# Stage B of a Fourier filter on 64x64 array tiles, with its loads and reads rearranged

## The chip, the core and the metric

The kernel runs on one core of a Trainium2 chip. The core has a matrix engine (TensorE, PE in the profile; PEld is its weight load), a vector engine (VectorE, DVE), a scalar engine (ScalarE, ACT), a general engine (GpSimd, POOL) and SyncE (SP), which here only issues transfers. Each engine works through its own list of instructions in order and waits on semaphores. Sixteen DMA engines move data; they take transfers from a queue fed by SyncE (q1 in the profile), one fed by GpSimd (q0), and others. TensorE's products land in PSUM, eight banks of 128 partitions by 512 f32. The metric is the time of one execution in microseconds (us) on the device; lower is better.

## What is computed

```
X = rfft(x, axis=1)                    # x: [8, 3008, 256] f32
y = irfft(X * (filt_r + 1j*filt_i))    # [8, 3008, 256]
t = y.reshape(24064, 256)
out = (relu(t @ w_gate) * (t @ w_val)) @ w_out      # d_ff = 1536
```

Eight batches of 3008 positions with 256 channels go through a global filter in frequency space. The 24064 rows that come out go through a gated feed-forward layer (FFN) of width 1536.

## The kernel before, in words

The Fourier transform of 3008 = 94 x 32 is split in two.

*Stage A* transforms over n1 (94 positions, folded by symmetry) and gives 96 rows (real and imaginary parts of 48 frequencies k1) for each of 32 n2. It writes them to Abuf in DRAM. Batches 0 and 1 do it with full matmuls (`items_a`, psA). Batches 2 to 7 load chunks of x (`load_chunk`, six DMAs for each of four chunks), fold them on GpSimd (`fold_chunk`, six additions or subtractions), and multiply them on sixteen 32x32 tiles of the array (`tiled_a`, psF): tiles of one matmul instruction each, with a `tile_position` that says which rows and columns of the array it uses.

*Stage B* reads Abuf back by frequency (`load_at`, `load_at_tiled`; the tile `at`), transforms over n2, multiplies by the filter and transforms back. One frequency k1 is a 64x64 matrix (32 complex numbers). There are 24 groups g, each with two such matrices on the diagonal of a 128x128 matrix, half of which is zero. `fwd` (in `items_b`) makes psX for two groups with two matmuls; DVE multiplies psX by the real and the imaginary filter (tt and uu); `inv`, two or three calls later, makes psD with four matmuls (I2t with tt, I2u with uu), ACT copies it to dsb, and after six groups SyncE writes dsb to Dbuf in DRAM.

*The last transform* over n1 is joined with the FFN: `load_d` reads Dbuf (dC, four n2 a read, eight reads a batch), and `item_c` makes psY, the FFN's input of 512 rows (a block), copied to yT by ACT and DVE.

*The FFN* takes 47 blocks. Each has 12 steps: `gv` makes psV and psG (two matmuls of 512 columns each); ACT copies psV to vsb, DVE makes prod = relu(psG) x vsb; `o_part` adds a third of an output tile of the block before (four matmuls of 256 columns, psO), copied to osb by ACT in steps 5 and 11 and written out by SyncE.

The order is written out by hand. A table `side` says at which step of the FFN loop which part of the filter of a later batch is put in, after that step's `gv` and `o_part`: `at_step(s, f)`. `end` is the step from which the rest of batch b is counted; it lies five steps before the `item_c` that needs its first rows, and 72 steps before the next batch's. Stage B of a batch starts at `sb0`, 30 steps before `end` (batch 1: step 19), with one `fwd` and one `inv` every second step. The step decides only the place in each engine's list. An instruction runs as soon as its engine has come to it and its waits are met.

PSUM has four tags of two banks: fft, psv, psg and pso. In the FFN loop, psX, psD and psY take turns on the two banks of fft; psV and psG have psv and psg; `tiled_a` takes one bank each of psv and psg and both of fft. SBUF tiles have a number of buffers (`bufs`); a tile waits for the last user of the buffer that it takes over.

Before the loop, stage A of batch 0 and its stage B run alone, then stage A of batch 1 begins inside stage B of batch 0 (`amid`). GpSimd loads the filters and the FFN's weights (`load_vg`, `load_o`). The matrices for stage B are made on the chip: DVE spreads a table into F2 (`place_forward`), TensorE turns F2 into I2t and I2t into I2u (`make_back`).

```
for s, z in ((2, 2), (9, 4), (14, 6)):
    at_step(s, lambda z=z: load_d(0, z, z + 2))
```

This puts the remaining reads of batch 0's Dbuf at steps 2, 9 and 14; batch 1's `load_at` stands at step 5, so behind the first of them in SyncE's list.

Of the kernel before, what the change touches and what calls it, by code (L numbers as in the profile page):

```python
# [41 lines left out]
def _tables():  # L42
# [3 lines left out]
    wa = np.zeros((128, NROW + 2))  # L46
    for a in range(2):
        wa[64 * a:64 * a + 64, NROW + a] = 1.0
# [7 lines left out]
    for hg in range(48):  # L56
        g, a = divmod(hg, 2)
        rows = slice(a * 64, a * 64 + 64)
        f = np.zeros((64, 64))
# [4 lines left out]
        wa[part, 2 * hg] = np.cos(th)  # L64
        if k1 not in (0, 47):
            wa[part, 2 * hg + 1] = -np.sin(th)
            m1[48 * a + g] = 2.0 * np.cos(th) / S
            m1[48 * a + 24 + g] = -2.0 * np.sin(th) / S
# [8 lines left out]
        else:  # L77
            m1[48 * a + g] = np.cos(th) / S
# [15 lines left out]
        f2[lo + 64 * a, g] = f  # L94
# [4 lines left out]
    col = 4 * (8 * (r % 4) + r // 4 % 8) + 2 * (r // 64) + r // 32 % 2  # L99
    perm = np.zeros((128, 128))  # L100
    perm[r, col] = 1.0
# [15 lines left out]
    tab = np.concatenate([f2.reshape(128, -1), perm, swap, own.reshape(128, -1), m1], 1)  # L117
    return wa.astype(np.float32), fold.reshape(128, 128).astype(np.float32), tab.astype(NBF16)
# [3 lines left out]
def kernel(  # L122
# [17 lines left out]
    NZ = 8  # L140
# [4 lines left out]
    wa_h, fold_h, tab_h = _tables()  # L145
# [14 lines left out]
    WA = pro.tile([128, NROW + 2], FP32)  # L160
    WF = consts.tile([128, 4, 32], FP32)
    M1 = consts.tile([NROW, N1], BF16)
    F2 = consts.tile([128, NG, 128], BF16)
    I2t = consts.tile([128, NG, 128], BF16)
    I2u = consts.tile([128, NG, 128], BF16)
# [20 lines left out]
    f2c = tabs[:, 0:NG * 64].rearrange("p (g f) -> p g f", f=64)  # L186
    perm, swap = tabs[:, NG * 64:NG * 64 + 128], tabs[:, NG * 64 + 128:NG * 64 + 256]

    def place_forward():
        for a in range(2):  # L190
            nc.vector.tensor_scalar(F2[:, :, a * 64:a * 64 + 64], f2c,
                                    WA[:, NROW + a:NROW + a + 1], None, op0=ALU.mult)
        nc.vector.tensor_copy(M1, tabs[:NROW, NG * 64 + 512:])

    def make_back(i, q):

        psI = ps.tile([128, 4, 128], FP32, tag=fft_tag(), name="psI")
        gs = slice(4 * q, 4 * q + 4)
        if i == 0:
            for j in range(4):  # L200
                nc.tensor.matmul(psI[:, j], F2[:, 4 * q + j, :], perm, start=True, stop=True)
        else:
            nc.tensor.matmul(psI, swap, I2t[:, gs, :], start=True, stop=True)
        copy = nc.scalar.copy if i == 1 else nc.vector.tensor_copy
        copy((I2t, I2u)[i][:, gs, :], psI)

    def place_own():

        for i, t in enumerate((I2t, I2u)):
            o = NG * 64 + 256 + i * 128  # L210
            nc.vector.tensor_copy(
                t[64:, NG - 2:, :].rearrange("p g (n a c) -> p g n a c", a=2, c=2)[:, :, :, 1, :],
                tabs[64:, o:o + 128].rearrange("p (g n c) -> p g n c", g=2, c=2))
# [54 lines left out]
    def items_a(b):  # L268

        def one(c, j, st):  # L270
            if j == 0:
                st["asb"] = sb.tile([128, NC2 * D], BF16, tag="asb", bufs=4, name="asb")
            psA = ps.tile([128, 512], FP32, tag=fft_tag(), name="psA")
            o = (c * NC2 % NX2) * D + j * 512
            nc.tensor.matmul(psA[0:NROW], WA[:, :NROW], XF[c * NC2 // NX2][:, o:o + 512],  # L275
                             start=True, stop=True)
            dst = st["asb"][:NROW, j * 512:(j + 1) * 512]
            nc.scalar.copy(dst, psA[0:NROW])
            if j == 3:
                nc.sync.dma_start(_ap(Abuf[b], c * NROW * NC2 * D, [[NC2 * D, NROW], [1, NC2 * D]]),  # L280
                                  st["asb"][:NROW])
# [7 lines left out]
    def load_chunk(b, j):  # L289

        xp = XP[(4 * b + j) % 3]
        for q in range(4):
            r, o = 32 * q, 8 * q + 2 * j
            nc.sync.dma_start(xp[r:r + 24, 0:4:2, :],
                              _ap(x, (b * N1 * N2 + o) * D,
                                  [[N2 * D, 24], [47 * N2 * D, 2], [1, 512]]))
        for i in range(2):
            nc.sync.dma_start(xp[:, 2 * i + 1, :],
# [3 lines left out]
    def fold_chunk(b, j):  # L302

        xp = XP[(4 * b + j) % 3]
        t = fs.tile([128, 2, 512], FP32, tag="fold", bufs=2, name="fold")
# [9 lines left out]
    def tiled_a(b, j):  # L315
# [8 lines left out]
        asf = sb.tile([128, NC2 * D], BF16, tag="asb", bufs=4, name="asb")  # L324
# [9 lines left out]
    def load_at_tiled(b):  # L334

        ats[b] = sb.tile([128, NG, D], BF16, tag="at", bufs=1, name="at")
        for rr in range(4):
            for e in range(2):
                nc.sync.dma_start(ats[b][32 * rr:32 * rr + 32, e:NG:2, :],
                                  _ap(Abuf[b], (48 * (rr % 2) + 24 * e + 12 * (rr // 2)) * N2 * D,  # L340
                                      [[D, 32], [N2 * D, 12], [1, D]]))

    GC = 6
    POOL_G = (4, 6, 10, 12, 16, 18)
# [8 lines left out]
    def items_b(b, amid=None):  # L353

        held = []
        st = {}
        lag = 2 if b else 3
        cuts = (0, 6, 12, 18, 24) if b else (0, 6, 12, 18, 22, 24)

        def fwd(g):  # L360
            at = ats[b]
            psX = ps.tile([128, 2, D], FP32, tag=fft_tag(), name="psX")
            for i in range(2):
                nc.tensor.matmul(psX[:, i], F2[:, g + i, :], at[:, g + i, :], start=True, stop=True)  # L364
            tt = sb.tile([128, 2, D], BF16, tag="tt", bufs=4)
            uu = sb.tile([128, 2, D], BF16, tag="uu", bufs=4)
            nc.vector.tensor_tensor(tt, psX, Ftr[:, g:g + 2, :], op=ALU.mult)  # L367
            if b == 0 and g in POOL_G:
                xs = pro.tile([128, 2, D], FP32, tag="xs", bufs=2)
                nc.scalar.copy(xs, psX)  # L370
                nc.gpsimd.tensor_tensor(uu, xs, Fti[:, g:g + 2, :], op=ALU.mult)  # L371
            else:
                nc.vector.tensor_tensor(uu, psX, Fti[:, g:g + 2, :], op=ALU.mult)  # L373
            held.append((g, tt, uu))

        def inv():
            g, tt, uu = held.pop(0)
            if g in cuts:
                st["dsb"] = sb.tile([128, GC, D], BF16, tag="dsb", bufs=4, name="dsb")
                st["g"] = g  # L380
            psD = ps.tile([128, 2, D], FP32, tag=fft_tag(), name="psD")
            for i in range(2):
                nc.tensor.matmul(psD[:, i], I2t[:, g + i, :], tt[:, i], start=True, stop=False)  # L383
                nc.tensor.matmul(psD[:, i], I2u[:, g + i, :], uu[:, i], start=False, stop=True)  # L384
            o = g - st["g"]
            nc.scalar.copy(st["dsb"][:, o:o + 2, :], psD)  # L386
            if g + 2 in cuts:
                nc.sync.dma_start(_ap(Dbuf[b], st["g"] * D, [[NG * D, 128], [1, (o + 2) * D]]),
                                  st["dsb"][:, :o + 2, :])

        for g in range(0, NG, 2):
            def both(g=g):
                fwd(g)
                if amid:
                    amid(g // 2)
                if len(held) > lag:
                    inv()
            yield both
        for _ in range(lag):
            yield inv  # L400
# [3 lines left out]
    def load_d(b, z0=0, z1=NZ):  # L404
        for z in range(z0, z1):
            dC = sb.tile([NROW, 4, D], BF16, tag="dC", bufs=12)
            nc.sync.dma_start(dC, _ap(Dbuf[b], z * 4 * NROW * D,
                                      [[D, NROW], [NROW * D, 4], [1, D]]))
# [14 lines left out]
    def item_c(k, h):  # L423
# [4 lines left out]
        for (o, b, n2, n1, w) in runs(k * W, W):  # L428
            nc.tensor.matmul(psY[:, o:o + w],  # L429
                             dCs[b, n2 // 4][:, n2 % 4, h * 128:(h + 1) * 128], M1[:, n1:n1 + w],  # L430
# [25 lines left out]
    def o_part(blk, s, prods):  # L456
# [9 lines left out]
        if s in (5, 11) or last and s % 3 == 2:  # L466
            t0 = t if last else t - 1
            osb = fs.tile([128, 2, D], FP32, tag="osb", bufs=5)
# [31 lines left out]
    load_x(0, nc.sync, ((0, 0, 2 * q), (0, 2 * q, 4 * q), (1, 0, 2 * q)))  # L500
    nc.sync.dma_start(tabs, nc.inline_tensor(tab_h, name="dft_tab").ap())
# [9 lines left out]
    place_forward()  # L511
    for i, f in enumerate(items_a(0)):
        f()
        if i >= 10:
            make_back(0, i - 10)
        else:
            warm(1, 256)
# [7 lines left out]
    for q in range(6):  # L525
        make_back(1, q)
        warm(3)
# [18 lines left out]
    for f in items_b(0, amid):  # L546
        f()
    load_d(0, 0, 2)
# [12 lines left out]
    def clear_chunks():  # L561
        for i in range(3):
# [9 lines left out]
    for s, z in ((2, 2), (9, 4), (14, 6)):  # L572
        at_step(s, lambda z=z: load_d(0, z, z + 2))
    C_AT = (8, 10)
    at_step(2, clear_chunks)
    for b in range(1, B):
        end = (b * S // W - 1) * NFT + C_AT[0] - 5
        sb0 = 19 if b == 1 else end - 30 | 1
        if b == 1:
            for c in range(4):  # L580
                at_step(5, lambda c=c: load_at(1, c))
        else:
            for j, (l, e) in enumerate(((-66, -41), (-60, -33), (-54, -27), (-40, -17))):
                at_step(sb0 + l, lambda b=b, j=j: load_chunk(b, j))
                at_step(sb0 + l + 1, lambda b=b, j=j: fold_chunk(b, j))
                at_step(sb0 + e, lambda b=b, j=j: tiled_a(b, j))
            at_step(sb0 + e + 4, lambda b=b: load_at_tiled(b))
# [45 lines left out]
```

## Time and profile before

| | us |
|---|---|
| median of 3 runs | 914.34 (913.85 to 916.62) |
| profiled execution | 913.1 |
| its span, first to last instruction | 911.3 |
| TensorE busy | 896.0 |
| VectorE busy | 578.0 |
| ScalarE busy | 500.8 |
| GpSimd busy | 262.4 |
| mean granted TensorE clock | 0.995 of full |

In the page's lists of groups a row gives the line of the kernel, the engine, the operation, what it writes and reads, its shape and how often it ran; then the busy time and the mean of one in ns; then how long the engine stood idle just before, and what ended that. In a timeline a row is start, length, engine, line, operation, tile and count, where equal rows that follow each other are merged. The chain of waits goes back from the last instruction to what released each one; its shares say which engine's work makes up the span. Durations of matmuls overlap, so how far apart they start says more than how long they take.

### The profile page before, as it was taken

Reading aid. Unit: us, or ns where it says so; the run is one execution under the profiler, and the core shown is the slowest. Engines: PE = TensorE matmul, PEld = TensorE weight load, DVE = VectorE, ACT = ScalarE, POOL = GpSimd, SP = SyncE. Lnnn points to the kernel's source line nnn. Section 1 sums busy time; section 2 is a strip of 40 time slices with the busy share of each in tenths; the row PEclk is TensorE's granted clock in tenths of the full one; section 3 lists DMA queues with packets and bytes.
Section 4 is the critical chain, followed back from the end, with each engine's and each line's share of the span. In section 5 each row is a group of like instructions: output and inputs, shape, how many; then the busy total and the mean of one; then the engine's idle time right before and its main releaser. Section 6 shows DMA issues by size and latency. Waiting matters only on the chain.

```text
span 911.3 us, 18044 instructions
## 1 busy us (share of the span) xinstructions
PE 896.0 (98%) x6602; PEld 545.7 (60%) x6602; DVE 578.0 (63%) x875; ACT 500.8 (55%) x893; POOL 262.4 (29%) x181
## 2 busy tenths in 40 slices
PE   8799999999999999999999999999999999999997
PEld 3445665666655666556655566556665566666665
DVE  3737766568655775657755587555865567655553
ACT  4675555555555555555555555555555555555552
POOL 4340174405451074400844017440355300000000
PEclk9899999999999999999999999999999999999999
DMA  9996336444355345452353433525446242231111
GB/s 254 256 252 143 116 122 166 111 90 138 122 153 105 82 150 139 119 117 84 129 168 94 115 111 118 165 76 121 115 134 166 65 106 66 85 78 36 36 31 51
DMA packets 106138, 109.04 MB, mean 120 GB/s; under 512 B 9794, under 2 KB 87362, under 8 KB 105410
## 3 DMA queue, kind: packets, MB, share of 16 engines
q1 hardware_dynamic: 101222, 103.77, 40.7%
q0 software_dynamic: 4512, 3.90, 2.8%
q8 instruction: 52, 0.85, 0.4%
q14 instruction: 36, 0.29, 0.1%
q10 hardware_dynamic: 316, 0.22, 0.1%
HBM read 61.94 MB, written 49.81 MB: 123 GB/s over the span
## 4 chain that ended last, share of the span: by engine, by line
PE 95%; DMA 3%; SPq 0%; ACT 0%; POOL 0%; DVE 0%; issue 0%; ACTq 0%; POOLq 0%
PE psV L445 27%; PE psG L445 27%; PE psO L464 26%; PE psF L321 3%; PE psA L275 3%; PE psY L429 2%; PE psD L383 2%; PE psD L384 2%; PE psX L364 2%; DMA XF<-in_x_dram 1%; DMA Abuf<-asb 1%; DMA at<-Abuf 0%; DMA out_dram<-osb 0%; SPq L178 0%; SPq L478 0%
## 5 line engine op out<-in xcount | busy, mean ns | idle before, releaser
L450 DVE SCALAR_TENSOR_TENSOR prod<-psG,vsb 128x512 bf16<-128x512 f32 x564 | 390.0, 692 | 274.6 <-ACT vsb L448 265.6
L448 ACT CAST vsb<-psV 128x512 bf16<-128x512 f32 x564 | 332.0, 589 | 244.7 <-PE psV L445 206.4
L445 PE MATMUL psV<-yT,WvT 128*128 128x512 bf16 x1128 | 335.9, 379 | 0.9 <-ACT yT L434 0.7
L464 PE MATMUL psO<-WoT,prod 128*128 128x256 bf16 x2256 | 336.4, 273 | 0.0
L445 PE MATMUL psG<-yT,WgT 128*128 128x512 bf16 x1128 | 335.3, 379 | 0.0
L464 PEld LDWEIGHTS <-prod 128*128 128x128 bf16 x2256 | 220.7, 98 | 143.4
L445 PEld LDWEIGHTS <-WgT 128*128 128x128 bf16 x1128 | 110.0, 98 | 133.8 <-issue 0.5
L307 POOL TENSOR_TENSOR fold<-XP 128x1024 f32<-128x1024 f32 x24 | 56.4, 2351 | 404.5 <-DMA out_dram<-osb 170.9
L445 PEld LDWEIGHTS <-WvT 128*128 128x128 bf16 x1128 | 102.3, 98 | 33.1 <-issue 20.9
L386 ACT CAST dsb<-psD 128x512 bf16<-128x512 f32 x96 | 55.9, 588 | 51.7 <-PE psD L384 50.0
L367 DVE TENSOR_TENSOR tt<-psX,Ftr 128x512 bf16<-128x512 f32 x96 | 65.2, 682 | 4.2 <-PE psX L364 4.2
L470 ACT COPY osb<-psO 128x512 f32<-128x512 f32 x92 | 53.9, 586 | 22.7 <-PE psO L464 20.3
L373 DVE TENSOR_TENSOR uu<-psX,Fti 128x512 bf16<-128x512 f32 x90 | 61.3, 681 | 0.0
L308 POOL TENSOR_TENSOR XP<-XP 128x1024 f32<-128x1024 f32 x24 | 56.4, 2349 | 1.9
L384 PE MATMUL psD<-uu,I2u 128*128 128x256 bf16 x192 | 47.6, 276 | 0.6 <-POOL uu L371 0.6
L383 PE MATMUL psD<-tt,I2t 128*128 128x256 bf16 x192 | 47.9, 276 | 0.0
L328 ACT CAST asb<-psF 128x512 bf16<-128x512 f32 x48 | 25.8, 589 | 32.5 <-PE psF L321 32.5
L328 DVE CAST asb<-psF 128x512 bf16<-128x512 f32 x48 | 30.9, 686 | 17.3 <-PE psF L321 14.5
L364 PE MATMUL psX<-at,F 128*128 128x256 bf16 x192 | 37.8, 281 | 3.9 <-DMA at<-Abuf 3.9
L436 DVE CAST yT<-psY 128x512 bf16<-128x512 f32 x47 | 32.0, 681 | 12.9 <-PE psY L429 12.9
L434 ACT CAST yT<-psY 128x512 bf16<-128x512 f32 x47 | 27.5, 586 | 22.7 <-PE psY L429 22.6
L429 PE MATMUL psY<-M,dC 96*128 96x94 bf16 (+18 forms) x604 | 37.5, 198 | 0.0
(64 smaller groups left out, 439.9 us busy)
## 6 DMA issues: line engine op xcount, KB each, us to landing
dC<-Dbuf SPq DMA_DIRECT2D x64, 192.0 KB
XP<-in_x_dram SPq DMA_DIRECT2D x48, 256.0 KB
Dbuf<-dsb SPq DMA_DIRECT2D x31, 384.0 KB
XP<-in_x_dram SPq DMA_DIRECT2D x96, 96.0 KB
Abuf<-asb SPq DMA_DIRECT2D x96, 96.0 KB
at<-Abuf SPq DMA_DIRECT2D x48, 192.0 KB
out_dram<-osb SPq DMA_DIRECT2D x70, 94.0 KB
XF<-in_x_dram SPq DMA_DIRECT2D x12, 256.0 KB
```

The costliest lines, as they stand in the source:

```text
L307: tt(t, xp[:, 0:2], xp[:, 2:4], op=ALU.add)
L308: tt(xp[:, 2:4], xp[:, 0:2], xp[:, 2:4], op=ALU.subtract)
L328: copy(asf[:, :, q, :], banks[q])
L364: nc.tensor.matmul(psX[:, i], F2[:, g + i, :], at[:, g + i, :], start=True, stop=True)
L367: nc.vector.tensor_tensor(tt, psX, Ftr[:, g:g + 2, :], op=ALU.mult)
L373: nc.vector.tensor_tensor(uu, psX, Fti[:, g:g + 2, :], op=ALU.mult)
L383: nc.tensor.matmul(psD[:, i], I2t[:, g + i, :], tt[:, i], start=True, stop=False)
L384: nc.tensor.matmul(psD[:, i], I2u[:, g + i, :], uu[:, i], start=False, stop=True)
L445: nc.tensor.matmul(pt[:, :W], w[:, h, ft * 128:(ft + 1) * 128], yt[:, h, :], start=(h == 0), stop=(h == 1))
L448: nc.scalar.copy(vsb, psV[:, :W])
L450: nc.vector.scalar_tensor_tensor(prod, in0=psG[:, :W], scalar=0.0, in1=vsb, op0=ALU.max, op1=ALU.mult)
L464: nc.tensor.matmul(psO[:, t % 2], prods[ft][:, t * 128:(t + 1) * 128], WoT[:, ft, :], start=(ft == 0), stop=(ft == NFT - 1))
```

## The change

- Stage B works on 64x64 array tiles. F2, I2t and I2u hold 64 columns a group instead of 128 half-empty ones. `fwd(b, i)` does four groups: for each of two halves m, four matmuls on the four quarters of the array, into two banks (psX for e = 0 and e = 1). `inv(b, i)` does four groups with sixteen matmuls into two banks of psv and psg. `product` makes one of the four products of a `fwd`.
- In the FFN loop a batch has seven such places instead of fourteen: for batches 2 to 7 at -40, -35, -28, -23, -16, -11 and -4 from `end`, for batch 1 at -35, -28, -25, -22, -16, -11 and -4. The four products go to that step and the three after it; `inv` of the four groups before stands right behind `fwd`.
- x chunks are loaded from GpSimd's queue, not SyncE's, into four buffers XP instead of three. All four loads and then all four folds stand together at -104 to -100.
- D is read 8 n2 at a time (four dC of two DMAs each, six buffers instead of twelve). dsb holds eight groups, so three writes a batch instead of four. `at` is read with four DMAs instead of eight.
- At the start of the loop, batch 1's `load_at` stands at step 3 and the second read of batch 0's D at step 4.
- F2 is loaded ready made; `make_back_t` and `make_back_u` replace `make_back`, and `place_forward` goes.
- Buffers: asb 4 to 3, dsb 4 to 3, osb 5 to 4, fold 2 to 3, tt and uu 4 to 5.

```diff
-    F2 = consts.tile([128, NG, 128], BF16)
+    F2 = consts.tile([128, NG, 64], BF16)
...
+    def make_back_t(q):
+        psI = [ps.tile([128, 4, 64], FP32, tag=fft_tag(), name="psI") for _ in range(2)]
+        for e in range(2):
+            for a in range(2):
+                for j in range(4):
+                    nc.tensor.matmul(psI[e][64 * a:64 * a + 64, j],
+                                     F2[64 * e:64 * e + 64, 12 * a + 4 * q + j, :],
+                                     perm[64 * e:64 * e + 64], start=True, stop=True,
+                                     tile_position=(64 * e, 64 * a))
...
-        xp = XP[(4 * b + j) % 3]
+        xp = XP[j]
...
-            nc.sync.dma_start(xp[r:r + 24, 0:4:2, :],
+            nc.gpsimd.dma_start(xp[r:r + 24, 0:4:2, :],
...
-            nc.sync.dma_start(xp[:, 2 * i + 1, :],
+            nc.gpsimd.dma_start(xp[:, 2 * i + 1, :],
...
+    def fwd(b, i, es=(0, 1)):
+        for e in es:
+            psXs[b, i, e] = ps.tile([128, 2, D], FP32, tag=fft_tag(), name="psX")
+        for m in range(2):
+            for e in es:
+                for a in range(2):
+                    j = 12 * a + 2 * i + m
+                    nc.tensor.matmul(psXs[b, i, e][64 * a:64 * a + 64, m],
+                                     F2[64 * e:64 * e + 64, j, :],
+                                     ats[b][64 * e:64 * e + 64, j, :], start=True, stop=True,
+                                     tile_position=(64 * e, 64 * a))
+
+    def product(b, i, e, k, pool=False):
+        psX = psXs[b, i, e]
+        p = sb.tile([128, 2, D], BF16, tag=("tt", "uu")[k], bufs=5, name=("tt", "uu")[k])
+        filt = (Ftr, Fti)[k][:, 4 * i + e:4 * i + 4:2, :]
...
+            nc.vector.tensor_tensor(p, psX, filt, op=ALU.mult)
+        tus[b, i, e, k] = p
+
+    def inv(b, i, tags=None, cuts=CUTS):
+        if i in cuts:
+            dsbs[b] = i, sb.tile([128, 2, 4, D], BF16, tag="dsb", bufs=3, name="dsb")
+        i0, dsb = dsbs[b]
+        psD = [ps.tile([128, 2, D], FP32, tag=tags[a] if tags else fft_tag(), name="psD")
+               for a in range(2)]
+        for m in range(2):
+            for k in range(2):
+                for a in range(2):
+                    for e in range(2):
+                        nc.tensor.matmul(psD[a][64 * e:64 * e + 64, m],
+                                         (I2t, I2u)[k][64 * a:64 * a + 64, 4 * i + 2 * m + e, :],
+                                         tus[b, i, e, k][64 * a:64 * a + 64, m],
+                                         start=(k == 0), stop=(k == 1),
+                                         tile_position=(64 * a, 64 * e))
+        o = 2 * (i - i0)
+        for a in range(2):
+            nc.scalar.copy(dsb[:, a, o:o + 2, :], psD[a])
...
-    for s, z in ((2, 2), (9, 4), (14, 6)):
-        at_step(s, lambda z=z: load_d(0, z, z + 2))
+    for s, z in ((4, 1), (9, 2), (14, 3)):
+        at_step(s, lambda z=z: load_d(0, z, z + 1))
...
-                at_step(5, lambda c=c: load_at(1, c))
+                at_step(3, lambda c=c: load_at(1, c))
...
-            for j, (l, e) in enumerate(((-66, -41), (-60, -33), (-54, -27), (-40, -17))):
-                at_step(sb0 + l, lambda b=b, j=j: load_chunk(b, j))
-                at_step(sb0 + l + 1, lambda b=b, j=j: fold_chunk(b, j))
-                at_step(sb0 + e, lambda b=b, j=j: tiled_a(b, j))
+            for j, (l, e) in enumerate(((-104, -74), (-103, -69), (-102, -62), (-101, -57))):
+                at_step(end + l, lambda b=b, j=j: load_chunk(b, j))
+                at_step(end - 100, lambda b=b, j=j: fold_chunk(b, j))
+                at_step(end + e, lambda b=b, j=j: tiled_a(b, j))
...
-        for i, f in enumerate(items_b(b)):
-            at_step(sb0 + 2 * i, f)
-        at_step(sb0 + 27, lambda b=b: load_d(b))
+        for i, l in enumerate((-35, -28, -25, -22, -16, -11, -4) if b == 1 else
+                              (-40, -35, -28, -23, -16, -11, -4)):
+            if i < 6:
+                at_step(end + l, lambda b=b, i=i: fwd(b, i))
+                for h in range(4):
+                    at_step(end + l + h, lambda b=b, i=i, h=h: product(b, i, h // 2, h % 2))
+            if i > 0:
+                at_step(end + l, lambda b=b, i=i: inv(b, i - 1, ("psv", "psg")))
+        at_step(end - 2, lambda b=b: load_d(b))
```

## The prediction

> **What bounds the kernel now.** I read the page's busy shares, then its chain of waits, then windows of the timeline around the places the diff touches.
>
> ```profile
> span 911.3 us, 18044 instructions
> ...
> PE 896.0 (98%) x6602; PEld 545.7 (60%) x6602; DVE 578.0 (63%) x875; ACT 500.8 (55%) x893; POOL 262.4 (29%) x181
> ...
> PE 95%; DMA 3%; SPq 0%; ACT 0%; POOL 0%; DVE 0%; issue 0%; ACTq 0%; POOLq 0%
> ...
> L367 DVE TENSOR_TENSOR tt<-psX,Ftr 128x512 bf16<-128x512 f32 x96 | 65.2, 682 | 4.2 <-PE psX L364 4.2
> ```
>
> TensorE is 95% of the chain, so a matmul fewer is time saved and a new wait of TensorE is time lost. One FFN step with stage B work, from TensorE's timeline:
>
> ```profile
> 202.17 0.38 PE L364 MATMUL psX<-at,F 128*128 128x256 bf16 x2
> 202.39 0.27 PE L383 MATMUL psD<-tt,I2t 128*128 128x256 bf16 x1
> ...
> 202.83 0.59 PE L445 MATMUL psV<-yT,WvT 128*128 128x512 bf16 x2
> ...
> 204.13 0.38 PE L445 MATMUL psV<-yT,WvT 128*128 128x512 bf16 x1
> ```
>
> Six stage B matmuls take 0.66 us (0.109 each); a bare step takes 1.30 (202.83 to 204.13). Stage A already uses array tiles (psF):
>
> ```profile
> 245.19 0.60 PE L464 MATMUL psO<-WoT,prod 128*128 128x256 bf16 x4
> ...
> 245.72 0.61 PE L321 MATMUL psF<-XP,WF 24*32 24x512 f32 x1
> ...
> 246.18 0.59 PE L321 MATMUL psF<-fold,WF 24*32 24x512 f32 x2
> ...
> 246.44 0.59 PE L321 MATMUL psF<-fold,WF 24*32 24x512 f32 x2
> 246.45 0.59 PE L321 MATMUL psF<-XP,WF 24*32 24x512 f32 x1
> 246.97 0.60 PE L445 MATMUL psV<-yT,WvT 128*128 128x512 bf16 x2
> ```
>
> The sixteen tiles do overlap. Getting in costs 0.09 us (four psO at 0.109 end at 245.63, psF starts at 245.72). So does getting out: an untiled f32 pass takes 0.43, so the last psF ends at 246.88 and psV starts at 246.97. A tile's second pass starts 0.45 after its first, 0.026 more than its stream.
>
> The start of the FFN loop: SyncE's queue and TensorE in the timeline,
>
> ```profile
> 61.74 1.14 SPq L407 DMA_DIRECT2D dC<-Dbuf  x2
> 63.04 9.54 SPq L350 DMA_DIRECT2D at<-Abuf  x4
> ```
> ```profile
> 69.67 0.39 PE L429 MATMUL psY<-M,dC 96*128 96x52 bf16 x6
> ```
>
> and packets by queue (q0 GpSimd's, q1 SyncE's) in 66 to 72.5 us, then in 72.5 to 80:
>
> ```profile
> q0 software_dynamic: 1284, 0.64, 71.5%
> q1 hardware_dynamic: 1449, 0.82, 56.3%
> ```
> ```profile
> q1 hardware_dynamic: 4111, 2.04, 116.0%
> ```
>
> The DMA engines are saturated here (their share is 1.11, 1.28 and 1.17 in 60 to 66, to 72.5 and to 80). Block 1's psY at 69.67 reads two dC of 192 KB that stand ahead of batch 1's four at reads; no wait shows.
>
> **Part by part.** The profiled run took 913.1 (span 911.3 and 1.8 around it); the median is 1.2 higher, 914.3. Differences are summed against the profiled run and moved to the median.
>
> *Tiles, batches 1 to 7.* Out go 72 matmuls a batch, 72 x 0.109 = 7.86 us. In come 48 + 96 quarter-array ones in 36 rounds of four, in 7 slots, each with entry and exit of 0.19 and about 0.02 of stagger: 1.44. A round lies between 0.109 (a full-array stream) and 0.218 (two tiles take turns). psF's rows lie far nearer the first, with 0.026 extra at worst; I take 0.120: 36 x 0.120 + 1.44 = 5.76, a gain of 2.10 a batch, **-14.7** over seven. At 0.109 it is -17.5, at 0.135 -10.9, at 0.218 +10.0.
>
> The weight loads have no row: psF's are 32 columns of f32, start 0.007 apart and overlap. The Trainium skill, "TensorEngine Tiling (Array Packing)", Restrictions and Gotchas, says that column tiling switches fast weight load off, and "TensorE: Matmul & The Clock Gate", LDWEIGHTS, gives columns / 1.2 ns. Four loads of 53 ns one after another would make an estimated round of 0.213, and the sum 942 instead of the forecast; no run here shows such a load.
>
> *Batches 2 to 7, the covers.* inv now takes a psv and a psg bank and two dsb copies fall in one step. ACT then owes vsb, at times osb, and two dsb, 4 x 0.59 = 2.36, against a step of 1.30 + 0.93, and catches up in the next step. DVE owes 5 x 0.69 + 4 x 0.68 = 6.2 in the shortest gap of five steps, where TensorE takes 7.4. Banks come free some 0.4 us early: 0. Gone, that cover would cost up to 0.3 a slot.
>
> *Batch 1* has gaps of three steps, twice (-28, -25, -22). There the fourth product stands on DVE in the same step as the next fwd, which needs its bank. From the first slot's step: ACT is in dsb until 3.45, so vsb ends at 4.0; then DVE, a start each 0.60 (as at 33.98, 34.59, 35.19), does prod, product, prod, product, prod, product until 7.75. TensorE is there at 6.3. Wait 1.5, twice: **+3.0** (0 to 4.4).
>
> *Block 1's dC reads move behind the at reads* (at_step 3 before at_step 4; both on SyncE's queue). TensorE comes to psY at step 8, at 69.7 as before, and now needs 3072 packets of at (4 x 384 KB by 512 B) and 768 of dC. By the window rows some 1400 of them have gone at 72.5, and the remaining 2440 at 4111 / 7.5 = 548 per us land at 77.0. That is the low end.
>
> *x loads on GpSimd's queue.* 144 issues leave SyncE (idle or waiting mostly; worth 0) and join GpSimd. Nothing holds them to their steps there: batch 2's 24 stand right behind four memsets (5.29 for three from 60.87, so done at 67.9) and start then, not near 100. They are 1792 packets of 2 KB, at some 0.6 us per issue (GpSimd's DMA rows are 0.50 to 0.75) until 82.3. In 66 to 72.5 the two queues got about equal turns (1284 and 1449 packets); with equal turns at the 314 GB/s of 60 to 66, 2.5 KB a pair and so 122 pairs per us, dC lands near 88. The ends are 77 and 88. The issue pace leaves gaps to q1, so I take 83, midway: TensorE stands still, **+13.3** against 69.7. Behind its waiting psY stand steps 9 to 11 and all of block 1, and ACT and DVE wait for those; batch 1's at, which lands before, is late for nobody.
>
> *Cold clock after that stall.* Before, after 3.93 us idle, TensorE ran at 0.50 from 33.4 to 38.6 us:
>
> ```profile
> 33.40:38.50 5.10, 5.10 (x27) 3.61 (x28) 4.52 (x8) 1.39 (x3) 2.36 (x4) 0.50 0.68 119
> ```
>
> 5.2 us at half is **+2.6**. The Trainium skill, "TensorE: Matmul & The Clock Gate", Part 1, has full rate back after one busy window of about 3.4 us. By that it would be an estimated 1.7 and the sum 0.9 lower.
>
> *asb with three buffers.* Batch 1's last chunk waits for its first chunk's write to land, near 62 (96 packets of 4 KB, begun at 60 behind the dC reads, at the 396 packets of 60 to 66), instead of a copy at 58.2. Four copies and yT later the FFN loop starts near 64.8 instead of 61.9. This +2.9 lies inside the stall above: 0; without the stall it counts.
>
> *Batch 0 and the tables.* F2 comes by DMA instead of two DVE multiplies (618 ns each, off the path). Six groups of four 128-column matmuls (0.22 each) become three tiled groups, 0.19 + 16 x 0.03: +0.4 before the Abuf write. Stage B of batch 0 after the x of batch 1 lands (43.75) loses six inv and two fwd at 0.11 a matmul for tiles: -0.4. Sum 0, within 0.5.
>
> *The rest at 0.* GpSimd's folds: 2 x 2.35 + 4 x 1.27 = 9.8 a chunk, with 3.6 for its loads 53 us a batch, where a batch lasts 110 (first psF 135.9 to 245.7). Loads wait for tiled_a of the batch before, folds stand behind them, and each fold still ends some five steps ahead of its tiled_a. D: last inv at 238.69, psY at 252.18; the write is 512 KB instead of 384 and two reads are needed, about 1 us later, with 2 us to spare and two psF more in between. at in four reads of the same bytes, osb with four buffers (a reuse every 31 us): unseen. If these covers go, TensorE waits at psF or psY once a batch.
>
> Sum: -14.7 + 3.0 + 13.3 + 2.6 = +4.2; 917.3 for the profiled run, **918.5** for the median.
>
> **Rivals.**
> - *The at and dC reads keep their pace beside the x loads* (dC at 77). For it: a DMA of GpSimd's waits for an older one, so few are in flight. Against: equal turns in 66 to 72.5. -14.7 + 3.0 + 7.3 + 2.6 = -1.8: 912.5.
> - *The other side, faster: block 1's reads are there by 72.6,* when TensorE arrives. -14.7 + 3.0 + 2.9 = -8.8: 905.5. It decides at 78.8 us: dC landing before that leaves a gain, after it a loss. Against: 3840 packets must pass first; for: only the queue's order, not the packets, is certain.
> - *Waits per slot in batches 2 to 7* (the fwd, bank or dsb cover gone): 36 slots x 0.3 = +11: 929. Against: 0.4 us in hand.
> - *The tiles take turns* (0.218 a round), the change does not do what it says: +24.7, 943. Against: psF.
>
> **How the numbers follow.** Forecast 0.48 (its own range 912 to 925), first rival 0.22, faster rival 0.13, slot waits 0.12, turns 0.05. From 906 to 929 leaves out about half of the faster rival, the turns and part of the slot waits, together under 0.2. 0.3% is 2.7 us, about what a measurement can tell: the forecast gives 0.01 faster, 0.15 same, 0.32 slower; the first rival 0.09, 0.10, 0.03; the faster one 0.12 and 0.01; the others are slower. Faster 0.22, same 0.26, slower 0.52.
>
> **What would show it.** Right: psY idle some 10 us for DMA dC between 70 and 85 us, GpSimd issuing XP loads from 68, PEclk low just after; two waits of psX for DVE's products in batch 1 of about 1.5; 24 tiles in 0.93 us from psO to psV. Wrong: no idle at psY near 72 (faster rival), rounds of 0.2, or TensorE waiting for banks, psF or psY in each batch.

## The result and the profile after

The changed kernel takes 946.62 us (median of 4 runs, 939.2 to 949.45), the one before 914.1 beside it: 1.0338 times as long, 95% interval 1.0270 to 1.0406. The direction was the forecast one; the forecast was 918.5, and the time lies 17.6 us above its range. The profiled execution took 944.06, its span 942.3 (31.0 more than before). The page's span, busy times and shares of the chain of waits, changed kernel:

```profile
span 942.3 us, 19150 instructions
...
PE 890.0 (94%) x7202; PEld 515.7 (55%) x7202; DVE 567.9 (60%) x873; ACT 497.0 (53%) x890; POOL 352.9 (37%) x326
...
PE 76%; DMA 13%; SPq 2%; DVE 1%; issue 1%; ACT 0%; DVEq 0%
PE psV L461 23%; PE psO L480 22%; PE psG L461 22%; DMA Abuf<-asb 6%; DMA at<-Abuf 4%; PE psF L320 3%; PE psD L390 2%; PE psY L445 2%; DMA dC<-Dbuf 2%; PE psX L361 2%; DMA out_dram<-osb 1%; SPq L422 1%; SPq L337 1%; SPq L329 0%; DVE prod L466 0%
```

TensorE fell from 95% of the chain to 76%, and transfers rose from 3% to 13%: Abuf's writes and the at reads, not dC, have the larger shares. TensorE's waits, changed kernel (total us, times, longest):

```profile
PE psY L445 <- DMA dC<-Dbuf: 22.5, 1, 22.5
PE psX L361 <- DMA at<-Abuf: 11.4, 5, 4.5
PE psX L361 <- DMA out_dram<-osb: 4.9, 3, 3.3
...
PE psX L361 <- DVE uu L376: 2.2, 2, 1.1
```

The first and the last line were forecast. The two in the middle are one thing: the first psX of a batch waits for all of `at`, and the profile names whichever transfer ended last; the 4.5 in the second line is batch 0's own first read, 3.9 in the kernel before. One of a batch's five places that hold 24 tiles, TensorE's timeline:

```profile
220.81 0.60 PE L480 MATMUL psO<-WoT,prod 128*128 128x256 bf16 x4
221.34 0.41 PE L361 MATMUL psX<-at,F 64*64 64x256 bf16 x8
221.59 0.28 PE L390 MATMUL psD<-tt,I2t 64*64 64x256 bf16 x4
221.69 0.28 PE L390 MATMUL psD<-uu,I2u 64*64 64x256 bf16 x4
221.80 0.28 PE L390 MATMUL psD<-tt,I2t 64*64 64x256 bf16 x4
221.91 0.28 PE L390 MATMUL psD<-uu,I2u 64*64 64x256 bf16 x4
222.12 0.60 PE L461 MATMUL psV<-yT,WvT 128*128 128x512 bf16 x2
```

Four quarter tiles start every 0.11 us, the pace of one full matmul before. Places of 24, 16 and 8 tiles without a wait last 0.875, 0.657 and 0.438 in all batches: 0.109 a round and 0.219 for getting in and out. A batch costs 5 x 0.875 + 0.657 + 0.438 = 5.47 instead of 7.86.

The start of the loop, TensorE's and then SyncE's timeline:

```profile
73.36 0.27 PE L445 MATMUL psY<-M,dC 96*128 96x52 bf16 x3
96.15 0.38 PE L445 MATMUL psY<-M,dC 96*128 96x94 bf16 x3 [22.52 <-DMA dC<-Dbuf]
96.33 1.06 PE L461 MATMUL psV<-yT,WvT 128*128 128x512 bf16 x2
```
```profile
65.49 8.07 SPq L347 DMA_DIRECT2D at<-Abuf  x4
73.61 18.80 SPq L422 DMA_DIRECT2D dC<-Dbuf  x6
```

TensorE stands from 73.6 to 96.15 (before: psY at 69.67 without a wait), then works at half rate until 101.0. A window behind the wait, with the busy times of PE, PEld, DVE, ACT and POOL, then granted clock, DMA share and GB/s:

```profile
96.30:101.00 4.70, 4.70 (x19) 1.93 (x18) 1.64 (x3) 1.75 (x3) 3.15 (x5) 0.50 1.11 199
```

Where the 31.0 went, by starts of matmuls in the two traces: block 1's psY goes on at 96.15 instead of 69.67, +26.5 (3.7 of it a later start of the loop, which the wait covers); half rate behind it for 4.9 us, +2.3; batch 1's two waits 1.42 and 1.33, +2.75; `at` late for the first psX of batches 2 to 6 by 2.67, 0.84, 4.46, 0.95 and 4.50, +13.4; half rate for 3.4 us behind each of the two longest, +3.4; tiles 7 x (7.86 - 5.47) = -16.7. The sum is +31.7.

Half of the loss was not in the forecast: the at reads of batches 2 to 6. SyncE's timeline around those of batch 4, and of batch 7, which has no later batch whose x must be loaded:

```profile
411.07 5.08 SPq L329 DMA_DIRECT2D Abuf<-asb  x4
425.29 2.19 SPq L337 DMA_DIRECT2D at<-Abuf  x4
```
```profile
743.73 1.95 SPq L329 DMA_DIRECT2D Abuf<-asb  x4
746.92 2.24 SPq L337 DMA_DIRECT2D at<-Abuf  x4
```

The last psF of batch 4 starts at 406.5 and its at reads 18.8 later, behind writes to Abuf that have not landed; for batch 7 it is 741.8 and 5.1. GpSimd issues batch 5's 24 x loads from 390.75 to 413.6, of which the first and the last rows are

```profile
390.75 2.33 POOL L293 DMA_DIRECT2D XP<-in_x_dram  x4
...
412.18 1.41 POOL L297 DMA_DIRECT2D XP<-in_x_dram  x2 [0.50 <-DMA XP<-in_x_dram]
```

and the last of them lands at 424.7 in the trace, just before the at reads go out. The DMA queues in 406.5 to 424 of the changed kernel show what the loads take (packets, MB, share of the engines):

```profile
q0 software_dynamic: 1525, 1.79, 59.1%
q1 hardware_dynamic: 707, 1.15, 27.1%
```

### The profile page after: what moved, and what is told of

Same layout as the page of the kernel before. It is cut to its first block, busy times and chain, and to the rows that moved or that the text cites. A ratio compares the mean times of both kernels' runs of the same rounds, so it can differ in the third digit from the quotient of the medians.

```text
span 942.3 us, 19150 instructions
## 1 busy us (share of the span) xinstructions
PE 890.0 (94%) x7202; PEld 515.7 (55%) x7202; DVE 567.9 (60%) x873; ACT 497.0 (53%) x890; POOL 352.9 (37%) x326
## 3 DMA queue, kind: packets, MB, share of 16 engines
q0 software_dynamic: 22176, 26.01, 15.0%
## 4 chain that ended last, share of the span: by engine, by line
PE 76%; DMA 13%; SPq 2%; DVE 1%; issue 1%; ACT 0%; DVEq 0%
PE psV L461 23%; PE psO L480 22%; PE psG L461 22%; DMA Abuf<-asb 6%; DMA at<-Abuf 4%; PE psF L320 3%; PE psD L390 2%; PE psY L445 2%; DMA dC<-Dbuf 2%; PE psX L361 2%; DMA out_dram<-osb 1%; SPq L422 1%; SPq L337 1%; SPq L329 0%; DVE prod L466 0%
## 5 line engine op out<-in xcount | busy, mean ns | idle before, releaser
L461 PEld LDWEIGHTS <-WvT 128*128 128x128 bf16 x1128 | 98.7, 98 | 43.5 <-issue 32.4
L293 POOL DMA_DIRECT2D XP<-in_x_dram x96 | 56.0, 586 | 53.5 <-DMA XP<-in_x_dram 19.5
L397 ACT CAST dsb<-psD 128x512 bf16<-128x512 f32 x96 | 51.5, 589 | 27.1 <-PE psD L390 27.1
L445 PE MATMUL psY<-M,dC 96*128 96x94 bf16 (+18 forms) x604 | 38.0, 199 | 22.5 <-DMA dC<-Dbuf 22.5
L445 PEld LDWEIGHTS <-dC 96*128 96x128 bf16 x604 | 34.9, 98 | 26.1 <-issue 23.8
L361 PE MATMUL psX<-at,F 64*64 64x256 bf16 x384 | 27.0, 298 | 18.5 <-DMA at<-Abuf 11.4
```

Of the source, the lines that this page charges most:

```text
L293: nc.gpsimd.dma_start(xp[r:r + 24, 0:4:2, :], _ap(x, (b * N1 * N2 + o) * D, [[N2 * D, 24], [47 * N2 * D, 2], [1, 512]]))
L397: nc.scalar.copy(dsb[:, a, o:o + 2, :], psD[a])
L445: nc.tensor.matmul(psY[:, o:o + w], dCs[b, n2 // 8][:, n2 % 8, h * 128:(h + 1) * 128], M1[:, n1:n1 + w], start=True, stop=True)
L461: nc.tensor.matmul(pt[:, :W], w[:, h, ft * 128:(ft + 1) * 128], yt[:, h, :], start=(h == 0), stop=(h == 1))
```

## The experiments

The first four ran beside the kernel before at 913.81, the next four at 913.63, the last three at 913.66. Spans and rows are those of the profiled execution of each.

**The reads in the order of before**

```diff
-    for s, z in ((4, 1), (9, 2), (14, 3)):
+    for s, z in ((2, 1), (9, 2), (14, 3)):
-                at_step(3, lambda c=c: load_at(1, c))
+                at_step(5, lambda c=c: load_at(1, c))
```

> The changed kernel with the reads at the start of the loop in the order of before (block 1's dC read at step 2, batch 1's at reads at step 5); the x loads stay on GpSimd's queue. Theory 'the x loads take the DMA engines': dC lands before TensorE is at psY (73.4 us), so the 22.5 us of psY go, but batch 1's at now ends the row of reads, near 94, and its first fwd, near 83, waits about 11 for it; the waits for at in batches 2 to 6 (13.4 together) stay. Span 942.3 - 22.5 - 2.4 + 11 + some 2 of cold clock = 930. Theory 'the order of the reads alone': no wait at psY and none at batch 1's psX, span 942.3 - 24.9 = 917, or 904 if the later waits go with it.

931.02 us, 1.0179 of before (1.0152 to 1.0205), span 929.4. TensorE's waits:

```profile
PE psX L361 <- DMA at<-Abuf: 20.8, 6, 10.3
PE psX L361 <- DMA out_dram<-osb: 3.1, 1, 3.1
...
PE psY L445 <- DMA dC<-Dbuf: 0.4, 1, 0.4
```

The wait moves from psY to batch 1's first psX (10.3 at 84.6 us), and the later ones stay, as the theory of the x loads has it: 929.4 against 930. Order alone is not the cause.

**The x loads on SyncE's queue**, with the reads as changed and then with both edits

```diff
-            nc.gpsimd.dma_start(xp[r:r + 24, 0:4:2, :],
+            nc.sync.dma_start(xp[r:r + 24, 0:4:2, :],
...
-            nc.gpsimd.dma_start(xp[:, 2 * i + 1, :],
+            nc.sync.dma_start(xp[:, 2 * i + 1, :],
```

> The changed kernel with the x loads on SyncE's queue, at the steps where the changed kernel puts them; the order of the reads stays that of the changed kernel. Theory 'the x loads take the DMA engines': without them the at and dC reads land near 79.5 (77 as forecast, and the loop's start is 2.5 us later), so psY waits about 6 instead of 22.5; the waits for at in batches 2 to 6 go (13.4, and about 3.4 of cold clock behind two of them). Span 942.3 - 16.5 - 13.4 - 3.4 = 909. Theory 'the order of the reads alone': psY still waits 20 or more and the at waits stay, span 940. Theory 'SyncE issues the at reads too late for batches 2 to 6': psY waits 6, the at waits stay, span 926.

> The changed kernel with both: reads in the order of before, x loads on SyncE's queue. Theory 'x loads and order together': no wait at psY, at lands near 80 and batch 1's first fwd comes near 83, no waits for at later; what is left against before is the gain of the tiles (16.7 by the slots' lengths), two waits of 1.4 in batch 1 and 3.7 us of a later start of the loop. Span 942.3 - 22.5 - 2.4 - 13.4 - 3.4 = 900.6, some 11 below before. If something else of the change costs time, the span stays above 905.

923.7 us, 1.0095 (1.0058 to 1.0132), span 923.4; with both, 913.43 us, 1.0000 (0.9981 to 1.0019), span 911.6. Waits of TensorE, one edit and then both:

```profile
PE psY L445 <- DMA dC<-Dbuf: 17.3, 5, 9.3
PE psX L361 <- DMA at<-Abuf: 4.5, 1, 4.5
```
```profile
PE psY L445 <- DMA dC<-Dbuf: 9.6, 5, 2.9
PE psX L361 <- DMA at<-Abuf: 4.5, 1, 4.5
```

The wait at 74 us falls from 22.5 to 9.3, and all waits for at in batches 2 to 6 are gone: so far as forecast. But both spans are 11 to 14 above their sums, because four of those batches now wait at psY, 8 us together; the rest is the wait at 74 us itself (9.3 for 6, and 1.7 for none) and half rate behind it or behind the later ones. SyncE comes later to the last Dbuf write and the dC reads behind it: batch 2's write is issued at 247.9, where the next kernel, shifted to the same block start, has it at 243.8; SyncE spent 17.6 us between 196 and 258 waiting at x loads and at output writes for x loads to land. At these steps, loads on SyncE's queue exchange one wait for another. The kernel before issues the same loads from SyncE at other steps, and its TensorE never waits for dC.

**The x loads on GpSimd's queue, but held**

```diff
+            at_step(end - 104, lambda b=b: hold_gpsimd(ats[b - 1][:, NG - 1, 0:8] if b > 2
+                                                       else dCs[0, 1][:, 7, 0:8]))
```

`hold_gpsimd` copies a few elements on GpSimd, which so waits for the transfer that writes them.

> The changed kernel with one small copy on GpSimd ahead of each batch's x loads, which waits for the at reads of the batch before (for batch 2: for block 1's dC); the loads stay on GpSimd's queue and start when those have landed. Theory 'the moment at which the x loads run': as with the loads on SyncE's queue, psY waits about 6 and the later at waits go, span near 909. Theory 'GpSimd's queue itself slows what runs beside it, whenever': waits of the same size appear elsewhere (dC, osb), span above 925.

913.17 us, 0.9989 (0.9978 to 1.0001), span 912.5. SyncE's timeline for batch 4 and the waits of TensorE:

```profile
391.77 1.52 SPq L329 DMA_DIRECT2D Abuf<-asb  x4
395.12 2.44 SPq L337 DMA_DIRECT2D at<-Abuf  x4
```
```profile
PE psY L445 <- DMA dC<-Dbuf: 5.7, 1, 5.7
PE psX L361 <- DMA at<-Abuf: 4.4, 1, 4.4
```

The at reads go out 5.2 us after the last psF (389.9), and batches 2 to 7 have no wait left. The psY wait is 5.7, 6 expected; the span is 3.5 above the sum. TensorE comes to psY 3.4 later than in the changed kernel: the loop starts at 66.7 instead of 65.6, after a wait of 4.3 for the first yT, and the clock is at half from 64.5 to 71.3, which costs 2.3. GpSimd's queue is not the trouble; the moment is.

**Order and hold together** (batch 2's loads held for batch 1's at)

> The changed kernel with the reads at the start in the order of before, and GpSimd's x loads held until the at reads of the batch before have landed (batch 2 too). Theory 'it is where the x loads run against the reads': the start of the run with both edits on SyncE (block 7 from 188.4 us) and the rest of the held run (912.5 - 199.1 = 713.4 from block 7 to the end): span 901.8, about 1.1% below before. Theory 'held loads only move the collision': with batch 1's at landing near 80, the x loads of batch 2 run over the dC reads for block 2, psY waits 3 or more there, span 905 or above.

904.12 us, 0.9895 (0.9878 to 0.9911), span 902.0 against 901.8:

```profile
PE psX L361 <- DMA at<-Abuf: 4.1, 1, 4.1
...
PE psY L445 <- DMA dC<-Dbuf: 1.7, 1, 1.7
```

The tiles' gain is there, and this version beats both kernels. The hold is all that differs from the first experiment, 929.4: the unheld x loads cost 27.4.

**One part of the change in the kernel before.** First the order of the reads alone:

```diff
-    for s, z in ((2, 2), (9, 4), (14, 6)):
+    for s, z in ((4, 2), (9, 4), (14, 6)):
-                at_step(5, lambda c=c: load_at(1, c))
+                at_step(3, lambda c=c: load_at(1, c))
```

> The kernel before with one part of the change alone: batch 1's at reads at step 3 and block 1's dC reads behind them at step 4; x loads stay on SyncE's queue. The prediction's low end has block 1's dC landing at 77.0 instead of 67: psY waits 7.3 at 69.7, and the clock falls for up to 2.6: span 911.3 + 7.3 to 9.9 = 918.6 to 921. Rival 'the at reads are no faster than the whole queue, so dC comes later': 9 or more of wait. Rival 'dC is there by 72.6': 914 or less.

923.59 us, 1.0105 (1.0087 to 1.0124), span 922.8:

```profile
PE psY L429 <- DMA dC<-Dbuf: 8.0, 1, 8.0
```

8.0 against 7.3, and half rate until 85.0, 6.1 us of it in work. dC is there at 78.9, the low end of the prediction had 77.0; the loop starts 0.9 later here, and the span is 1.8 above the upper end of what was expected. So the low end holds within 2 us. Then `load_chunk` on GpSimd's queue alone:

> The kernel before with one part of the change alone: x chunks are loaded from GpSimd's queue (three buffers, loads and folds one after the other as before). Theory 'it is the 24 loads together, right behind the folds, that meet the reads': here a fold stands between two loads of six, the reads get through, no wait for at or dC beyond 1 us, time within 0.3% of before. Theory 'loads from GpSimd's queue take the DMA engines from SyncE's reads, however placed': waits for at in batches 1 to 6 of some 2 each and at psY, 10 or more in all.

916.62 us, 1.0031 (1.0017 to 1.0045), at the edge of the 0.3%. One wait appears, 1.9 at batch 1's first psX (83.7 us), which neither theory had; batches 2 to 7 have none. So loads from GpSimd's queue can run without stopping the reads. Whether the folds between them, the three buffers or the other steps see to that, this run does not separate.

**Batch 1's places five steps apart** (on order and hold)

```diff
-        for i, l in enumerate((-35, -28, -25, -22, -16, -11, -4) if b == 1 else
+        for i, l in enumerate((-35, -30, -25, -20, -15, -10, -4) if b == 1 else
```

> As the kernel with the order of before and held x loads, and batch 1's places at -35, -30, -25, -20, -15, -10 and -4 from end, so that no gap is of three steps. Theory 'batch 1's two waits come from the fourth product of the fwd three steps before': both waits of psX for uu go, every slot of 24 tiles lasts 0.875, 2.75 less. Rival 'they come from DVE's load as such': a wait remains in one or more of the slots, less than 1.5 gained.

905.2 us (two runs), span 903.0, 1.0 more than without. All 24-tile places last 0.875 now, so the cause was the fourth product. But the product is now late for psY, which takes the other use of the same two banks:

```profile
PE psY L445 <- DVE uu L376: 3.1, 2, 1.6
```

Two stops of about 1.7 replace two of about 1.4; the rest of the 1.0 is a loop that starts 0.3 later.

**Four buffers of asb, two of fold** (on the spaced kernel)

> As the spaced kernel, with four buffers of asb and two of fold instead of three and three. Theory 'the third buffer of asb delays the start of the loop': the wait of ACT for Abuf's write (2.6 in the changed kernel) goes, and the loop starts 1.5 to 2.6 earlier than in the spaced kernel. Rival 'the start waits for the weights or for the cold clock': the loop starts within 0.5 of the spaced kernel. The third and fourth folds of a batch stand 0 to 1 us ahead of their tiled_a, so a wait of psF for the folds may give some of it back.

903.61 us, 0.9890 (0.9875 to 0.9904). ACT's wait for Abuf's write, 3.8 in the spaced kernel, is gone, and the loop starts at 63.54 instead of 65.20: 1.7 from the third buffer by this pair. (The start varies: seven runs with three buffers and the same work ahead of the loop have 64.45 to 66.72.) A half-rate stretch of 3.4 us at the start of the spaced kernel's loop goes too. Later folds cost nothing that can be seen. A wait for dC of 1.7 and one for WgT of 0.6 take most of it back (span 902.3).

**The half-rate clock before the loop.** In the changed kernel the loop starts 3.7 us late; some 1.7 of it is asb. Windows of before (the first two rows), then of the changed kernel, over batch 0's stage B:

```profile
33.40:38.60 5.20, 5.20 (x27) 3.61 (x28) 4.62 (x8) 1.49 (x3) 2.46 (x4) 0.50 0.70 120
38.60:43.70 5.10, 3.04 (x27) 2.31 (x25) 4.04 (x7) 4.10 (x9) 3.94 (x5) 1.00 1.10 353
```
```profile
33.40:43.80 10.40, 10.38 (x97) 4.96 (x97) 8.06 (x13) 4.78 (x9) 6.15 (x7) 0.50 0.88 236
43.80:49.80 6.00, 6.00 (x31) 1.93 (x29) 1.98 (x3) 3.30 (x7) 2.31 (x2) 0.50 0.98 330
49.80:56.00 6.20, 6.20 (x45) 2.72 (x45) 1.29 (x2) 5.33 (x11) 0.00 (x0) 1.00 0.50 176
```

Full-array matmuls bring the clock back after 5.2 us. Tiles, busy for all of 10.4 us, do not; it comes back 6 us into the full-array psA. Two edits to tell why: the nine junk matmuls between the tiles with 512 columns instead of 128 (on the spaced kernel), and 18 more junk matmuls in the idle time ahead of stage B (on order, hold, and four buffers of asb with two of fold).

> As the spaced kernel, and the nine junk matmuls between the tiles of batch 0's stage B have 512 columns instead of 128. Theory 'tiles count for less than full-array matmuls in what raises TensorE's clock': the half-rate stretch from about 33 us, 13.7 to 17.1 us long in the runs with tiles against 6.8 before, falls to 6.8 or 10.2, psA runs at 0.43 a pass and the FFN loop starts 1 to 2 us earlier. Rival 'the length of the stretch has nothing to do with the tiles': it stays at 13.7 or 17.1, and the junk itself (9 x 0.32 at half rate) makes the loop start up to 2.9 later.

907.76 us (two runs). The stretch became 20.5 us long (30.8 to 51.2, the tiles from 33.7), and the loop started at 68.30, 3.1 later than at 65.20. Neither side had that length: more full-array work among the tiles did not bring the clock back.

> The changed kernel with the reads in the order of before, held x loads, batch 1's places as the change has them, four buffers of asb and two of fold, and 18 more junk matmuls (3.9 us) after the last of the table, so that TensorE stands idle for 1 to 2 us instead of 4.6 before batch 0's stage B. Theory 'the half-rate stretch comes from the idle time, and TensorE was short of nothing else': no half rate between 32 and 50, psA at 0.43 a pass from the start, the loop starts 1 to 2.3 earlier than at 63.5. Theory 'the tiles with their short pauses keep the clock down, whatever went before': TensorE falls to half rate during the tiles all the same, and the loop starts at 63.5 within 0.5. Total by the sum of the parts: 902.0 (reads in order, loads held) - 1.3 (asb) = 900.7 of span, less the gain of the clock.

902.49 us, 0.9873 (0.9856 to 0.9891), span 900.5 against 900.7: the fastest version run, with batch 1's places as the change has them. Its windows from the first tile on:

```profile
34.20:37.70 3.50, 3.06 (x41) 1.66 (x42) 3.04 (x6) 0.00 (x0) 1.61 (x3) 1.00 0.69 75
37.80:44.50 6.70, 5.95 (x60) 2.79 (x55) 4.82 (x8) 4.81 (x9) 4.53 (x4) 0.50 1.03 327
44.50:48.00 3.50, 3.44 (x7) 0.97 (x8) 1.53 (x3) 2.20 (x5) 2.30 (x2) 0.50 1.01 361
48.10:54.00 5.90, 5.90 (x63) 2.70 (x62) 1.64 (x3) 5.10 (x10) 0.00 (x0) 1.00 0.76 252
```

The tiles begin at full rate, after 1.22 us of idle, and lose it at 37.8, among the tiles; it comes back 3.4 us into psA. The loop starts at 63.89 (63.54 without the junk). So the low clock comes with the tile stage even without the idle time ahead of it. Two waits of 0.4 and 0.6 lie around its fall, so this does not show what property of the stage it is: pauses at changes of tiles, or the half-used array of each psX there. That stays open.

## Why the prediction was wrong

- *Tiles, -14.7:* right in kind, -16.7 measured. A round took 0.109, the low end; entry and exit of 0.19 held. The estimate of 0.213 a round, worked out from the Trainium skill ("TensorEngine Tiling (Array Packing)", Restrictions and Gotchas), is contradicted by every place.
- *Batch 1, +3.0:* 2.75, two waits of psX for DVE's fourth product, as worked out.
- *dC behind the at reads and beside x loads, +13.3:* the step had the right mechanism and half the size: dC landed at 96.1, not 83. The order alone was sized within 2 us (in the kernel before, dC was there at 78.9, 77.0 forecast). The term that failed is the rate beside x loads, even at its slow end of 88: it took "equal turns" at 314 GB/s, 122 pairs of packets per us, from a stretch where SyncE's queue moved 4 KB packets. In 80 to 90 us of the changed kernel (packets, MB, share):

```profile
q0 software_dynamic: 845, 1.13, 72.1%
q1 hardware_dynamic: 962, 0.48, 39.4%
```

  The turns are about equal, but there are 85 to 96 per us, at 162 GB/s. The Trainium skill, "DMA: Bandwidth & Descriptors", Issuing engines are not separate DMA queues, says that such transfers interleave on the same engines, which agrees with these rows. The x loads are also 2944 packets a batch with a mean of 1.25 KB (q0 has 22176 packets in the changed kernel, 4512 before), not 1792 of 2 KB; with that count the forecast's own 122 pairs per us give 92.5 instead of 88. The at reads started 2.5 later (65.5 against 63.0). And "until 82.3" was wrong for the loads: they began at 70.3, and GpSimd, waiting for its own older transfers, issued the last at 99.4, so the competition lasted the whole wait.
- *Cold clock, +2.6:* 2.3, 4.9 us at half after the wait; behind the long waits of four other runs (reads in order, x loads on SyncE, held, and the order alone in the kernel before) it was 3.8 to 6.1. The Trainium skill's 3.4 us of work until full rate ("TensorE: Matmul & The Clock Gate", Part 1) is short of all of these, and for batch 0's tiles does not hold: 10.4 us at half, busy throughout.
- *asb with three buffers, 0:* right, the later start lies inside the wait; without that wait it counts 1.7 by the one pair measured, not 2.9.
- *Batch 0 and the tables, 0 within 0.5:* wrong by about 2 (3.7 less 1.7). The longer half-rate stretch lies there, but no run shows how much of the 2 it makes. The wait covers it here.
- *The rest at 0, "at in four reads of the same bytes ... unseen":* the step that failed most, 13.4 and 3.4 of half rate behind it. The prediction saw that the next batch's loads wait for `tiled_a` of the batch before, and weighed them against GpSimd's folds only. They are let go by that same `tiled_a`, and so run while its results are written to Abuf and read back; held until the at reads had landed, they cost none of this. It allowed a wait at psF or psY if a cover went; it came at psX.
- *Rivals:* none happened. The first (dC at 77) underrated the loads like the forecast did; slot waits in batches 2 to 7 stayed away, and the tiles did not take turns.

By the prediction's own terms: -16.7 + 2.75 + 26.5 + 2.3 + 16.8 = +31.7, against +4.2 forecast and 31.0 in the spans.

## What to carry to other kernels

A transfer moved to a queue that nothing paces starts as soon as its buffer is free. Ask which event frees the buffer: if it is the event that also sends out transfers someone is waiting for, both run at once, and the one awaited loses; a hold until what must land first has landed gained 27.4 us here, the other queue 17.8 (929.4 to 911.6). Take a rate for two competing queues from a stretch with the packet sizes that will compete. And when a wait is removed or spaced out, follow the shared buffer or bank to its next user: here psY took over the waits of psX, and dC those of at.

## What was not expected of the hardware

Four 64x64 tiles run at the pace of one full matmul (0.109 us for 256 columns), with 0.219 for getting in and out of a stretch. Around batch 0's stage B, TensorE's granted clock was at half for 10.2 to 20.5 us in all ten kernels with tiles, where the three with full matmuls there (before and its two variants) did so for 3.4 to 6.8; once it fell from full rate among the tiles. Why the waits for at alternate between about 0.9 and 4.5 from batch 3 to 6 stays open.
